# Weight transfers at time 0, first one-hot rows by VectorE, high halves and 1/z products by GpSimd, z transfers on the SyncE queue

## The chip, the cores and the metric

The kernel runs on one core of one Trainium2 chip. The metric is the device time in microseconds (us) of one execution; smaller is better. Times quoted are medians of the timed runs. "Span" is the length of the one execution that was profiled. It is about 2 us below that run's time, and it can be one of the faster or slower runs.

Engine names: PE is TensorE, ACT is ScalarE, DVE is VectorE, POOL is GpSimd and SP is SyncE. A "q" after the name (SPq) means the engine's instruction queue, which issues transfers.

## The reference

Attention restricted to clusters, followed by an MLP with SiLU. Every query and key is assigned to one of 16 centroids of its head, and a query sees only keys of its own cluster.

```python
# q, k, v: (4, 8, 768, 64); centroids: (8, 16, 64); w_in: (512, 2048); w_out: (2048, 512), all float32
q_assign = argmax(einsum('bhsd,hcd->bhsc', q_n, c_n), -1)      # q_n, k_n, c_n: normalised
k_assign = argmax(einsum('bhsd,hcd->bhsc', k_n, c_n), -1)
mask = q_assign[:, :, :, None] == k_assign[:, :, None, :]
scores = where(mask, (q @ k.T) / sqrt(64), -1e9)
attn = exp(scores - max(scores)); attn /= sum(attn) + 1e-9
x = (attn @ v) as (3072, 512)                                   # 3072 tokens
h = x @ w_in;  g = h * sigmoid(h);  out = g @ w_out
```

## The kernel before

The mask is part of the score matmul. Q and K are turned so that the 64 features lie on partitions 0 to 63, and 16 more partitions (64 to 79) hold the one-hot cluster rows. One matmul over 80 partitions gives the score plus a large constant where the clusters agree. Each number is split into two f16 numbers, a high half and a low half (`hl`), and the two are transposed together: for the first four pairs of heads by PE, for the later pairs by a transposing DMA.

The work is a list of 144 slots. A slot is one score tile (`st`), one exp (`P`) and later one product with V (`pv`). The 16 pairs of heads, four per batch, take nine slots each. MoE matmuls (`ph`, `po`) start once a batch has finished a third of its tokens; they fill PE from then on. Each engine carries out its instructions in program order, and so does each queue that issues DMAs.

```python
def cast_v(p):                                   # V to f16, by GpSimd
    for h in range(2):
        nc.gpsimd.tensor_copy(vts[p % NV][:, :, h, 0:D], natvs[p][:, h]...)

def split(p, t, part, eng=nc.vector):            # t: 0 for q, 1 for k
    if part == 0:                                # L94: high halves
        eng.tensor_scalar(out=hl[:, :, 0, :], in0=nat, scalar1=128.0, scalar2=None, op0=ALU.mult)
    else:                                        # L97: low halves
        nc.vector.scalar_tensor_tensor(out=hl[:, :, 1, :], in0=nat, scalar=128.0, in1=hl[:, :, 0, :], ...)

def turn_dma(p, t):                              # L107
    nc.sync.dma_start_transpose(abt_of(p)[:, t], hls.pop((p, t)).rearrange("p a c d -> p (a c d)"))

# ... logits (PE), route_a to route_d (DVE): transpose, max, compare, transpose, scale -> one-hot rows oh
def route_e(pl):                                 # L176: one-hot rows into place, by DMA
    for a, p in enumerate(pl):
        for h in range(2):
            for t in range(2):
                nc.sync.dma_start(ab[D : D + HC, h, :], oh[g : g + HC, :])

# the sum of exps (z) of one slot triple: to 32 partitions, 1/z, to DRAM, broadcast to 64 partitions
def z_out(n):    nc.gpsimd.dma_start(zt, osbs[n][D : D + 1]...)
def z_recip(n):  nc.vector.reciprocal(rz, zts.pop(n)); nc.gpsimd.dma_start(rzd..., rz)
def z_bcast(n):  nc.gpsimd.dma_start(rzb..., rzs.pop(n).to_broadcast([64, 2 * UQ]))
def z_mul(n, p, u):                              # L235: products with 1/z
    for h in range(2):
        nc.vector.tensor_tensor(out=xts[c]..., in0=osb[0:D, h, :], in1=rzb[:, h, :], op=ALU.mult)

# ... the weights: 16 casting DMAs (f32 in DRAM, f16 in SBUF) on GpSimd's queue, one per two slots
for n in range(2):
    for r in range(NR):
        wld.append(lambda r=r, o=o: nc.gpsimd.dma_start(win_s[:, r, o], win_v[:, r, o]))
for g in range(NFB // 2):
    wld.append(lambda g=g: nc.gpsimd.dma_start(wout_s[:, 2 * g : 2 * g + 2], wout_v[:, 2 * g : 2 * g + 2]))
# ...
for n, fn in enumerate(wld):
    at(1 + 2 * n, fn)
```

The softmax here doesn't subtract the row's maximum and nothing guards it: scores larger than these inputs give would overflow.

Of the kernel before, what the change touches and what calls it, by code (L numbers as in the profile page):

```python
# [17 lines left out]
def kernel(  # L18
# [41 lines left out]

    wh = const.tile([128, HB, 2, 32], f16, name="wh")
    wl = const.tile([128, HB, 2, 32], f16, name="wl")
    NV = 6
    vts = [const.tile([128, NJ, 2, 128], f16, name=f"vt{n}") for n in range(NV)]

# [14 lines left out]
    def load_v(p):  # L80
        b, r = divmod(p, HB)
        natv = mp.tile([128, 2, NJ * D], f32, name="natv", bufs=2)
        nc.sync.dma_start(natv, v[b, 2 * r : 2 * r + 2].rearrange("h (p j) d -> p h (j d)", j=NJ))
        natvs[p] = natv
# [2 lines left out]
        for h in range(2):  # L87
            nc.gpsimd.tensor_copy(vts[p % NV][:, :, h, 0:D], natvs[p][:, h].rearrange("p (j d) -> p j d", d=D))

    def split(p, t, part, eng=nc.vector):  # L90
        nat = nats[p, t].rearrange("p h (j d) -> p (h j) d", d=D)
        if part == 0:
            hl = hls[p, t] = mp.tile([128, 2 * NJ, 2, D], f16, name="hl", bufs=3)
            eng.tensor_scalar(out=hl[:, :, 0, :], in0=nat, scalar1=128.0, scalar2=None, op0=ALU.mult)  # L94
        else:
            hl = hls[p, t]
            nc.vector.scalar_tensor_tensor(  # L97
                out=hl[:, :, 1, :], in0=nat, scalar=128.0, in1=hl[:, :, 0, :], op0=ALU.mult, op1=ALU.subtract
            )
# [76 lines left out]
                    nc.sync.dma_start(ab[D : D + HC, h, :], oh[g : g + HC, :])  # L176


    K = D + HC

    def qk(n, s, p, u):
# [28 lines left out]

    def z_out(n):
        zt = mp.tile([32, 16], f32, name="zt", bufs=3)
        nc.gpsimd.dma_start(zt, osbs[n][D : D + 1].rearrange("o h x -> o (h x)").rearrange("o (p i) -> o p i", p=32))  # L213
        zts[n] = zt

    def z_recip(n):
        rz = mp.tile([32, 16], f32, name="rz", bufs=2)
        nc.vector.reciprocal(rz, zts.pop(n))  # L218
        rzd = dr.tile([1, 2 * UQ], f32, name="rzd", bufs=4)
        nc.gpsimd.dma_start(rzd.rearrange("o (p i) -> (o p) i", p=32), rz)  # L220
        rzs[n] = rzd

    def z_bcast(n):
        rzb = mp.tile([64, 2, UQ], f32, name="rzb", bufs=4)
        nc.gpsimd.dma_start(rzb.rearrange("p h x -> p (h x)"), rzs.pop(n).to_broadcast([64, 2 * UQ]))  # L225
        rzbs[n] = rzb

    def z_mul(n, p, u):
        b, r = divmod(p, HB)
        c = b * U + u  # L230
        if c not in xts:
            xts[c] = mp.tile([128, NR, UQ], f16, name="xt", bufs=5)
        osb, rzb = osbs.pop(n), rzbs.pop(n)
        for h in range(2):
            nc.vector.tensor_tensor(  # L235
                out=xts[c][D * h : D * h + D, r, :], in0=osb[0:D, h, :], in1=rzb[:, h, :], op=ALU.mult
            )

# [52 lines left out]
    def centroid_rest(craw):  # L291
# [12 lines left out]
            nc.vector.tensor_scalar(out=ch2[:, n, :], in0=chh, scalar1=OHV, scalar2=None, op0=ALU.mult)  # L304
        for n in range(2):
            nc.vector.scalar_tensor_tensor(out=cl2[:, n, :], in0=cn, scalar=OHV, in1=ch2[:, n, :], op0=ALU.mult, op1=ALU.subtract)
        for src, dst in ((ch2, wh), (cl2, wl)):
            pt = ps.tile([128, 128], f16, name="pt", tag="moe", bufs=3)
            nc.tensor.transpose(pt, src.rearrange("p n d -> p (n d)"), ident)
            pt4 = pt.rearrange("p (r h c) -> p r h c", h=2, c=HC)  # L310
            for h in range(2):
                nc.vector.tensor_copy(dst[:, :, h, HC * h : HC * h + HC], pt4[:, :, h])


    units = []
# [11 lines left out]
        events.setdefault(slot, []).append(fn)  # L327


    nc.vector.memset(zbias, 0.0)  # L330
    nc.vector.memset(bias32, -32.0)
    craw = load_centroids()
    for p in range(2):
        for t in range(2):
            load(p, t)
    make_identity(nc, ident)
    nc.vector.memset(wh, 0.0)
    nc.vector.memset(wl, 0.0)
    for vt in vts:
        nc.gpsimd.memset(vt[:, :, :, D:128], 1.0)  # L340
    load_v(0)
    AC, VE = nc.scalar, nc.vector
    centroid_norm(craw)
    for t in range(2):
        split(0, t, 0, VE)
        split(0, t, 1)
# [1 line left out]
        for h in range(2):  # L348
            turn_pe(0, t, h, AC)
    for t in range(2):  # L350
        split(1, t, 0)
    centroid_rest(craw)
    logits([0])
    for t in range(2):
        load(2, t)
    load_v(1)
    split(1, 0, 1)
    route_a([0])
    route_b([0])
    route_c([0])  # L360
    route_d([0])
    route_e([0])
    cast_v(0)
    split(1, 1, 1)
    for t in range(2):
        for h in range(2):
            turn_pe(1, t, h, AC)

    wld = []
    for n in range(2):  # L370
        for r in range(NR):
            o = slice(n * DF // 2, (n + 1) * DF // 2)
            wld.append(lambda r=r, o=o: nc.gpsimd.dma_start(win_s[:, r, o], win_v[:, r, o]))
    for g in range(NFB // 2):
        wld.append(lambda g=g: nc.gpsimd.dma_start(wout_s[:, 2 * g : 2 * g + 2], wout_v[:, 2 * g : 2 * g + 2]))


    def route(pl, x):
# [25 lines left out]
    route([1], 1)  # L404
    front_pe(2, 2)
    front_pe(3, 9)
    at(0, lambda: cast_v(1))
    at(0, lambda: (load(3, 0), load(3, 1), load_v(2)))
    at(3, lambda: load_v(3))
    at(6, lambda: cast_v(2))  # L410
    at(8, lambda: cast_v(3))
    for n, fn in enumerate(wld):
        at(1 + 2 * n, fn)
    for b in range(1, B):
        front([b * HB, b * HB + 1], 36 * b - (3 if b == 1 else 8))
        front([b * HB + 2, b * HB + 3], 36 * b + (4 if b == 1 else 2))
# [88 lines left out]
```

## Time and profile before

| | before |
|---|---|
| time, median of the first 3 runs (range) | 393.85 us (393.36 to 396.67) |
| span of the profiled run | 390.8 us |
| first MoE matmul | 116.2 us |
| from there to the end | 274.6 us |
| exp of slot 0, 17, 24, 36 starts at | 23.8, 52.3, 77.8, 105.4 us |
| first eight transposes: first issue to last landing | 55.5 to 102.7 us |

Windows of the kernel before. Each row is a stretch of time: its length, the busy time (and instruction count) of PE, PE's weight loads, DVE, ACT and POOL, then PE's granted clock, the mean busy share of the 16 DMA engines, and GB/s.

```profile
core 0: us, PE busy (x) PEld busy (x) DVE busy (x) ACT busy (x) POOL busy (x), PEclk, DMA share, GB/s
0.00:52.00 52.00, 34.19 (x278) 24.05 (x278) 33.51 (x70) 28.93 (x32) 17.98 (x36) 0.80 0.58 149
52.00:78.00 26.00, 10.38 (x72) 7.05 (x72) 15.61 (x28) 7.96 (x9) 9.45 (x16) 0.73 1.13 208
78.00:116.00 38.00, 24.36 (x207) 17.11 (x206) 22.62 (x41) 18.91 (x18) 14.96 (x28) 0.86 0.87 156
106.00:380.00 274.00, 265.79 (x2116) 198.16 (x2115) 179.81 (x334) 175.43 (x204) 66.67 (x131) 0.99 0.38 103
```

In the last row PE is busy 266 of 274 us at a granted clock of 0.99: that part is bound by PE, and faster transfers could win at most the 8 us in which PE is idle. In the second row PE is busy only 10 of 26 us, while the DMA engines have no free time (a share above 1 means that packets' times overlap on an engine).

What PE waited for in the kernel before (total us, times, longest wait):

```profile
PE st L186 <- DMA abt<-oh: 24.3, 10, 11.6
PE ptt L113 <- DVE hl L97: 11.0, 3, 6.2
```

The largest wait is for the DMA that puts the one-hot rows into place. But that DMA is small, and it is only the last step of a chain. The chain of work that ended last (start, us, what), cut to its long pieces in the front:

```profile
2.67 6.06 DMA nat_93<-in_k_dram
...
18.70 3.88 DMA abt<-oh
...
53.25 3.68 DMA abt<-oh
...
71.56 3.11 SPq L107
74.72 5.06 DMA nat_789<-in_q_dram
79.79 13.02 DMA abt<-hl
```

`abt<-hl` is a transposing DMA. It took 13.0 us to land, and SyncE needed 3.1 us to issue one. The group of the first eight of these transposes, in the same trace (durations are SyncE's issue in ns; the second line is from issue to landing):

```profile
L107 SPq DMA_TRANSPOSE abt<-hl x8: 2073/4082/6230, 55.5 to 96.1; - x8
...
DMA to landing us min/median/max: 6.6/10.4/13.0
```

So the front can be read as three pieces that add up to the first MoE matmul: the stretch of the eight transposes begins (55.5 us), lasts (47.2 us), and 13.5 us later the first MoE matmul runs (116.2 us).

Of the work that the change moves, the products with 1/z are one group. Its columns are the number of instructions, busy us and mean ns, and the idle time before them with its cause.

```profile
L235 DVE TENSOR_TENSOR xt<-osb,rzb 64x256 f16<-64x256 f32 x96 | 40.6, 423 | 3.3 <-DMA rzb<-rzd 2.6
```

The high halves (L94) stand in the listing one by one, each with its own buffer; the median takes VectorE 0.55 us, and one takes 0.56 us in the chain.

### The profile page before, as it was taken

To read this page: it belongs to the slowest core of one execution; us is meant where nothing else is said; L and a number is where in the kernel's file an instruction comes from. 1 tells how busy PE (TensorE), PEld (TensorE's weight loads), DVE (VectorE), ACT (ScalarE), POOL (GpSimd) and SP (SyncE) were. 2 spreads that over 40 slices of the span, in tenths; PEclk is the share of its full clock that TensorE was granted. 3 is DMA by queue.
4 is the path that set the end of the run, shared out by engine and by line. 5 is a ranking of instruction groups with operands and counts; after the bars stand their busy time and mean duration, and the time that the engine had idled before them with its cause. 6 is when DMAs were issued, how large, how long until landed. Compare 5 with 4: busy or idle time off the path is not lost.

```text
span 390.8 us, 6883 instructions
## 1 busy us (share of the span) xinstructions
PE 336.5 (86%) x2658; PEld 245.4 (63%) x2658; DVE 248.0 (63%) x464; ACT 226.0 (58%) x255; POOL 106.0 (27%) x204
## 2 busy tenths in 40 slices
PE   2476965183849999999999999999999999999995
PEld 2345644162538877677777776777776777776572
DVE  6827577465554796796755786785845364555661
ACT  5157655054456776574776766665667666663350
POOL 5305162353420314223213133133221313122200
PEclk9668798588887999999999999999999999999999
DMA  7663589999716179654034598645120111111111
GB/s 250 128 200 70 118 164 219 199 243 181 145 45 206 30 190 267 136 138 102 20 118 154 137 245 216 137 101 96 49 68 16 55 42 49 48 43 54 68 42 55
DMA packets 65072, 47.35 MB, mean 121 GB/s; under 512 B 44048, under 2 KB 59408, under 8 KB 65040
## 3 DMA queue, kind: packets, MB, share of 16 engines
q1 hardware_dynamic: 56336, 36.22, 36.7%
q0 software_dynamic: 8704, 10.69, 13.5%
q8 instruction: 21, 0.34, 0.4%
q14 instruction: 11, 0.09, 0.1%
HBM read 33.59 MB, written 6.39 MB: 102 GB/s over the span
## 4 chain that ended last, share of the span: by engine, by line
PE 69%; DVE 12%; DMA 10%; issue 4%; SPq 3%; ACT 2%; DVEq 0%; ACTq 0%
PE ph L246 20%; PE po L260 19%; PE pv L201 14%; PE st L186 13%; DMA abt<-oh 4%; DMA abt<-hl 3%; PE psL L130 3%; DVE hl L97 2%; DMA nat_93<-in_k_dram 2%; DVE oht L155 1%; DVE mx L148 1%; SPq L176 1%; DMA nat_789<-in_q_dram 1%; DVE xt L235 1%; DVE ohu L164 1%
## 5 line engine op out<-in xcount | busy, mean ns | idle before, releaser
L190 ACT ACTIVATE P<-st,bias_70 128x1024 f16<-128x1024 f32 x144 | 158.1, 1115 | 93.8 <-PE st L186 93.1
L186 PE MATMUL st<-abt 80*128 80x256 f16 x576 | 92.2, 284 | 25.8 <-DMA abt<-oh 24.3
L251 DVE SCALAR_TENSOR_TENSOR gt<-tn,ph 128x512 f16<-128x512 f32 x96 | 64.9, 678 | 76.8 <-ACT tn L250 76.5
L246 PE MATMUL ph<-xt,win_s 128*128 128x256 f16 x768 | 99.4, 275 | 2.5 <-DVE lt L140 0.9
L260 PE MATMUL po<-wout_s,gt 128*128 128x512 f16 x384 | 96.0, 379 | 0.0
L250 ACT ACTIVATE tn<-ph,zbias 128x512 f32<-128x512 f32 x96 | 65.6, 684 | 47.4 <-PE ph L246 45.7
L186 PEld LDWEIGHTS <-abt 80*128 80x128 f16 x576 | 56.8, 101 | 46.4 <-DMA abt<-oh 27.0
L246 PEld LDWEIGHTS <-win_s 128*128 128x128 f16 x768 | 75.8, 99 | 15.2 <-issue 3.8
L220 POOL DMA_DIRECT2D rzd<-rz x48 | 25.1, 522 | 158.0 <-DVE rz L218 151.4
L260 PEld LDWEIGHTS <-gt 128*128 128x128 f16 x384 | 37.4, 97 | 28.5
L207 DVE COPY osb<-pv 128x512 f32<-128x512 f32 x48 | 32.5, 676 | 21.2 <-PE pv L201 21.2
L225 POOL DMA_DIRECT2D rzb<-rzd x48 | 25.1, 522 | 68.3 <-DMA rzd<-rz 68.3
L235 DVE TENSOR_TENSOR xt<-osb,rzb 64x256 f16<-64x256 f32 x96 | 40.6, 423 | 3.3 <-DMA rzb<-rzd 2.6
L213 POOL DMA_DIRECT2D zt<-osb x48 | 24.0, 501 | 30.4 <-DVE osb L207 30.1
L201 PE MATMUL pv<-P,vt_77 128*128 128x256 f16 x108 | 17.3, 304 | 5.5 <-DVE osb L207 5.5
L263 DVE TENSOR_SCALAR ot<-po 128x512 f32<-128x512 f32 x24 | 16.1, 669 | 7.8 <-PE po L260 7.8
L113 PE MATMUL ptt<-ident,hl 128*128 128x128 f16 x96 | 9.9, 266 | 11.0 <-DVE hl L97 11.0
L201 PEld LDWEIGHTS <-vt_77 128*128 128x128 f16 x108 | 11.7, 108 | 10.0 <-issue 5.7
L201 PE MATMUL pv<-P,vt_75 128*128 128x256 f16 x108 | 16.1, 289 | 0.0
L116 ACT COPY abt<-ptt 128x768 f16<-128x768 f16 x12 | 9.2, 805 | 11.5 <-PE ptt L113 11.5
L113 PEld LDWEIGHTS <-hl 128*128 128x128 f16 x96 | 8.0, 121 | 12.6 <-DVE hl L97 12.0
L140 DVE STREAM_TRANSPOSE lt<-psL 128x512 f32<-128x512 f32 (+1 forms) x10 | 7.1, 709 | 13.8 <-PE psL L130 13.8
(128 smaller groups left out, 272.3 us busy)
## 6 DMA issues: line engine op xcount, KB each, us to landing
natv<-in_v_dram SPq DMA_DIRECT2D x16, 384.0 KB, 5.7
rzb<-rzd POOLq DMA_DIRECT2D x48, 128.0 KB, 2.9
out_dram<-ot SPq DMA_DIRECT2D x24, 256.0 KB, 2.2
win_s<-in_moe_w_in_dram POOLq DMA_DIRECT2D x8, 256.0 KB, 5.2
wout_s<-in_moe_w_out_dram POOLq DMA_DIRECT2D x8, 256.0 KB, 8.8
abt<-oh SPq DMA_DIRECT2D x64, 24.0 KB, 2.0
zt<-osb POOLq DMA_DIRECT2D x48, 2.0 KB, 2.1
rzd<-rz POOLq DMA_DIRECT2D x48, 2.0 KB, 1.8
```

What stands on the lines that cost most here:

```text
L186: nc.tensor.matmul(st[:, a, h, :], ab[0:K, 1, h, ts(2 * s + a, 128)], ab[0:K, 0, h, ts(u, UQ)], start=True, stop=True)
L190: nc.scalar.activation(out=P, in_=st, func=AF.Exp, bias=bias32, scale=ESC)
L201: nc.tensor.matmul(po[:, h, :], vts[p % NV][:, 2 * s + a, h, :], P[:, a, h, :], start=(s == 0 and a == 0 and h == 0), stop=(s == 2 and a = ...
L207: nc.vector.tensor_copy(osb, po)
L213: nc.gpsimd.dma_start(zt, osbs[n][D : D + 1].rearrange("o h x -> o (h x)").rearrange("o (p i) -> o p i", p=32))
L220: nc.gpsimd.dma_start(rzd.rearrange("o (p i) -> (o p) i", p=32), rz)
L225: nc.gpsimd.dma_start(rzb.rearrange("p h x -> p (h x)"), rzs.pop(n).to_broadcast([64, 2 * UQ]))
L235: nc.vector.tensor_tensor(out=xts[c][D * h : D * h + D, r, :], in0=osb[0:D, h, :], in1=rzb[:, h, :], op=ALU.mult)
L246: nc.tensor.matmul(ph[:, e, :], win_s[:, r, ts(2 * f + e, 128)], xts[c][:, r, :], start=(r == 0), stop=(r == NR - 1))
L250: nc.scalar.activation(out=tn, in_=ph, func=AF.Tanh, bias=zbias, scale=0.5)
L251: nc.vector.scalar_tensor_tensor(out=gts[c][:, 2 * f : 2 * f + 2, :], in0=tn, scalar=1.0, in1=ph, op0=ALU.add, op1=ALU.mult)
L260: nc.tensor.matmul(po, gts[c][:, fc, ts(s, 128)], wout_s[:, fc, :], start=(fc == 0), stop=(fc == NFB - 1))
```

## The change

The intent is to take the weight transfers out of the saturated stretch (part 1), to take a DMA out of the way to the first scores (part 2), to relieve VectorE by giving elementwise work to GpSimd (part 3), and to free GpSimd's queue of the z transfers so that it can do that work (part 4).

```diff
-    def split(p, t, part, eng=nc.vector):
+    def split(p, t, part, eng=nc.gpsimd):                    # part 3
@@ ...
+    def route_first():                                       # part 2: rows of pair 0
+        ...   # logits with 32 columns per (q/k, head), of which 16 are used; transpose; max; compare; transpose
+        for h in range(2):
+            for t in range(2):
+                g = 64 * h + 32 * t
+                nc.vector.tensor_scalar(out=ab[D : D + HC, h, :], in0=ohu[g : g + HC, :], scalar1=OHV, ...)
@@ z_out, z_recip, z_bcast
-        nc.gpsimd.dma_start(...)
+        nc.sync.dma_start(...)                               # part 4
@@ z_mul
-            nc.vector.tensor_tensor(
+            nc.gpsimd.tensor_tensor(                         # part 3
@@ main
     centroid_norm(craw)
+    for r in range(NR):                                      # part 1: eight DMAs of twice the size
+        nc.gpsimd.dma_start(win_s[:, r], win_v[:, r])
+    for g in range(NFB // 4):
+        nc.gpsimd.dma_start(wout_s[:, 4 * g : 4 * g + 4], wout_v[:, 4 * g : 4 * g + 4])
@@ ...
     for t in range(2):
         load(2, t)
     load_v(1)
+    for t in range(2):
+        load(3, t)
+    split(1, 0, 0, AC)                                       # pair 1's high halves by ScalarE
+    split(1, 1, 0, AC)
     centroid_rest(craw)
     split(1, 0, 1)
-    route_a([0]) ... route_e([0])
+    route_first()
     cast_v(0)
+    for vt in vts[2:]:
+        nc.gpsimd.memset(vt[:, :, :, D:128], 1.0)
+    cast_v(1)
+    load_v(2)
+    load_v(3)
@@ ...
-    for n, fn in enumerate(wld):
-        at(1 + 2 * n, fn)
```

Two smaller things go with the four parts: ScalarE makes pair 1's high halves, and pair 3's q and k are loaded earlier.

More of the change, by code (lines that the diff above doesn't have):

```diff
@@ L62 @@
     wl = const.tile([128, HB, 2, 32], f16, name="wl")
+    w0 = const.tile([128, 2, 32], f16, name="w0")
     NV = 6
@@ L93, in split @@
             hl = hls[p, t] = mp.tile([128, 2 * NJ, 2, D], f16, name="hl", bufs=3)
-            eng.tensor_scalar(out=hl[:, :, 0, :], in0=nat, scalar1=128.0, scalar2=None, op0=ALU.mult)
+            if eng is nc.scalar:
+                nc.scalar.mul(hl[:, :, 0, :], nat, 128.0)
+            else:
+                eng.tensor_scalar(out=hl[:, :, 0, :], in0=nat, scalar1=128.0, scalar2=None, op0=ALU.mult)
         else:
@@ L176, in route_e @@
                     nc.sync.dma_start(ab[D : D + HC, h, :], oh[g : g + HC, :])
+    oht0 = mp.tile([128, S], f16, name="oht", bufs=1)
+    def route_first():
+        tl = []
+        for lo, hi in ((0, 512), (512, 768)):
+            psL = ps.tile([128, 512], f32, name="psL", tag="moe", bufs=3)
+            for i, w in enumerate((wh, wl)):
+                for h in range(2):
+                    for t in range(2):
+                        g = 64 * h + 32 * t
+                        ab = abts[0][:, t].rearrange("p (h j) c -> p h (j c)", h=2)
+                        nc.tensor.matmul(
+                            psL[g : g + 32, 0 : hi - lo], w0[:, i] if h else w[:, 0, 0], ab[:, h, lo:hi],
+                            start=(i == 0), stop=(i == 1),
+                        )
+            tl.append(psL)
+        lt = mp.tile([128, S], f32, name="lt", bufs=1)
+        nc.vector.transpose(lt[:, 0:512], tl[0])
+        nc.vector.transpose(lt[:, 512:768], tl[1][:, 0:256])
+        l3 = lt.rearrange("p (a c) -> p a c", c=32)[:, :, 0:HC]
+        mx = mp.tile([128, S // 32], f32, name="mx0")
+        nc.vector.tensor_reduce(out=mx, in_=l3, axis=AX.X, op=ALU.max)
+        oht = oht0
+        nc.vector.tensor_tensor(
+            out=oht.rearrange("p (a c) -> p a c", c=32)[:, :, 0:HC], in0=l3,
+            in1=mx.unsqueeze(2).to_broadcast([128, S // 32, HC]), op=ALU.is_ge,
+        )
+        ohu = mp.tile([128, S], f16, name="ohu", bufs=1)
+        nc.vector.transpose(ohu, oht)
+        for h in range(2):
+            for t in range(2):
+                g = 64 * h + 32 * t
+                ab = abts[0][:, t].rearrange("p (h j) c -> p h (j c)", h=2)
+                nc.vector.tensor_scalar(
+                    out=ab[D : D + HC, h, :], in0=ohu[g : g + HC, :], scalar1=OHV, scalar2=None, op0=ALU.mult
+                )
     K = D + HC
@@ L212, in z_out @@
         zt = mp.tile([32, 16], f32, name="zt", bufs=3)
-        nc.gpsimd.dma_start(zt, osbs[n][D : D + 1].rearrange("o h x -> o (h x)").rearrange("o (p i) -> o p i", p=32))
+        nc.sync.dma_start(zt, osbs[n][D : D + 1].rearrange("o h x -> o (h x)").rearrange("o (p i) -> o p i", p=32))
         zts[n] = zt
@@ L219, in z_recip @@
         rzd = dr.tile([1, 2 * UQ], f32, name="rzd", bufs=4)
-        nc.gpsimd.dma_start(rzd.rearrange("o (p i) -> (o p) i", p=32), rz)
+        nc.sync.dma_start(rzd.rearrange("o (p i) -> (o p) i", p=32), rz)
         rzs[n] = rzd
@@ L224, in z_bcast @@
         rzb = mp.tile([64, 2, UQ], f32, name="rzb", bufs=4)
-        nc.gpsimd.dma_start(rzb.rearrange("p h x -> p (h x)"), rzs.pop(n).to_broadcast([64, 2 * UQ]))
+        nc.sync.dma_start(rzb.rearrange("p h x -> p (h x)"), rzs.pop(n).to_broadcast([64, 2 * UQ]))
         rzbs[n] = rzb
@@ L306, in centroid_rest @@
             nc.vector.scalar_tensor_tensor(out=cl2[:, n, :], in0=cn, scalar=OHV, in1=ch2[:, n, :], op0=ALU.mult, op1=ALU.subtract)
-        for src, dst in ((ch2, wh), (cl2, wl)):
+        for i, (src, dst) in enumerate(((ch2, wh), (cl2, wl))):
             pt = ps.tile([128, 128], f16, name="pt", tag="moe", bufs=3)
@@ L312, in centroid_rest @@
                 nc.vector.tensor_copy(dst[:, :, h, HC * h : HC * h + HC], pt4[:, :, h])
+            nc.vector.tensor_copy(w0[:, i, 0:HC], pt4[:, 0, 1])
     units = []
@@ L327, in at @@
         events.setdefault(slot, []).append(fn)
+    AC, VE = nc.scalar, nc.vector
     nc.vector.memset(zbias, 0.0)
@@ L335 @@
             load(p, t)
+    load_v(0)
     make_identity(nc, ident)
@@ L338 @@
     nc.vector.memset(wl, 0.0)
-    for vt in vts:
+    nc.vector.memset(w0, 0.0)
+    nc.vector.memset(oht0, 0.0)
+    for vt in vts[0:2]:
         nc.gpsimd.memset(vt[:, :, :, D:128], 1.0)
-    load_v(0)
-    AC, VE = nc.scalar, nc.vector
     centroid_norm(craw)
+    for r in range(NR):
+        nc.gpsimd.dma_start(win_s[:, r], win_v[:, r])
+    for g in range(NFB // 4):
+        nc.gpsimd.dma_start(wout_s[:, 4 * g : 4 * g + 4], wout_v[:, 4 * g : 4 * g + 4])
     for t in range(2):
@@ L350 @@
     for t in range(2):
-        split(1, t, 0)
-    centroid_rest(craw)
-    logits([0])
-    for t in range(2):
         load(2, t)
     load_v(1)
-    split(1, 0, 1)
-    route_a([0])
-    route_b([0])
-    route_c([0])
-    route_d([0])
-    route_e([0])
-    cast_v(0)
+    for t in range(2):
+        load(3, t)
+    split(1, 0, 0, AC)
+    split(1, 1, 0, AC)
+    centroid_rest(craw)
+    split(1, 0, 1)
+    route_first()
+    cast_v(0)
+    for vt in vts[2:]:
[3 more added lines that the diff above has]
+    load_v(3)
     split(1, 1, 1)
@@ L367 @@
             turn_pe(1, t, h, AC)
-    wld = []
-    for n in range(2):
-        for r in range(NR):
-            o = slice(n * DF // 2, (n + 1) * DF // 2)
-            wld.append(lambda r=r, o=o: nc.gpsimd.dma_start(win_s[:, r, o], win_v[:, r, o]))
-    for g in range(NFB // 2):
-        wld.append(lambda g=g: nc.gpsimd.dma_start(wout_s[:, 2 * g : 2 * g + 2], wout_v[:, 2 * g : 2 * g + 2]))
     def route(pl, x):
@@ L406 @@
     front_pe(3, 9)
-    at(0, lambda: cast_v(1))
-    at(0, lambda: (load(3, 0), load(3, 1), load_v(2)))
-    at(3, lambda: load_v(3))
     at(6, lambda: cast_v(2))
     at(8, lambda: cast_v(3))
-    for n, fn in enumerate(wld):
-        at(1 + 2 * n, fn)
     for b in range(1, B):
```

## The prediction

> **What bounds the kernel now.** The table of busy time by stretch splits the span in two. From 120 us PE is busy 263 of 271 us at full clock: bound by PE. Before 116 us (first MoE matmul) it is busy 69 us, 47 idle. In the table of waits the largest idle is for abt<-oh (the one-hot rows' DMA): 24.3 us, 11.6 of it at 64-76 us. PE's work after 116 us is the same in both kernels, so what shortens the front shortens the whole.
>
> **What holds the front.** From 60 to 100 us the DMA share is 1.2: saturated. By the DMA packets of the trace, three weight DMAs (256 KB written each) kept the queue full from 15.5 to 22 us, 2 us each, so all 16 cost about 32 us. Eight (w_out) were issued at 53-97 us, among eight transposes (2 us of DMA each when alone). Estimate for 55-103 us: weights 16, transposes 16, loads 10, 1/z broadcasts 6 = 48 us: all of it.
>
> **The change.**
> 1. Weights at time 0: the 32 us now compete with the first loads. The Trainium skill ("DMA: Bandwidth & Descriptors", Queues, rings and completion order) says that each DMA engine takes queue rows in turn, by packet. The trace agrees roughly: at 38-42 us both queues got about half. So pair 1's q/k land about 3 us later (11-12 instead of 8.7), weights end near 46 us, and pair 1's one-hot DMA is slowed by 1-2 us. In return 16 us leave the saturated stretch, and the 3 us wait at 53-56 us goes. Gain about 13 us.
> 2. First one-hot rows by VectorE: removes DMA issue and landing at 18.0-22.6 us and halves the reduce and compare (0.95 us each); adds four copies (0.36 us each, as oh<-ohu). But PE must still turn pair 1 first. First st matmul at about 19.5 instead of 22.6: gain 3 us.
> 3. VectorE loses xt (40.6 us) and the high halves (0.55 us x 28): in the front 2-4 us of the routing chain, later off the chain. GpSimd gains them: high halves about 1.0 us (cast of 384 columns: 0.5 us); products by the skill ("GPSIMD Engine Reference", Elementwise — side-by-side cycle accounting, 2.6 cycles per element) an estimated 0.65-0.75 us, against 0.42 on VectorE. It loses 74 us of z issues.
> 4. z transfers on SyncE: 144 issues of about 0.5 us join, in order, transposes (1.3-6 us each in the front) and one-hot DMAs (0.55 us each); GpSimd's products, waiting, block its next high halves. This takes back 2-4 us in the front. After 120 us slack hides it. At the tail the last product ended just as PE needed it: loss 0-1 us.
>
> **Sum.** First MoE matmul at about 97 us; rest unchanged at 275 us; span 372 us; timed about 375 us (timed runs are 2-3 us above the span). Range 365 to 386. Chances: faster 0.85, within 2% 0.13, slower 0.02.
>
> **What would show it.** 1: no weight packets after 50 us; transposes landing in under 5 us in the front; the wait for abt<-oh under 10 us. 2: first st matmul at 18-21 us. 3: xt on GpSimd 0.6-0.9 us, VectorE busy near 190 us. 4: SyncE's waits before z transfers grow; PE over 95% busy after the first MoE matmul.
>
> **What would make it wrong.** Weight packets starving the first loads (start later than 23 us); SyncE's order making z latency pace the front, so that freed DMA time is not used; GpSimd products far over 1 us; or ScalarE's exp (1.1 us a slot) as the next floor, for a larger gain.

## The result, and the profile after

The ratio is the mean time of the changed kernel's fast runs over that of the kernel before's fast runs of the same rounds, so it is not quite the ratio of the medians.

| | before | after |
|---|---|---|
| time, median of 4 runs (range) | 395.26 (393.36 to 397.34) | 381.84 (381.10 to 382.93) |
| ratio, 95% interval | | 0.9662 [0.9597, 0.9726] |
| span | 390.8 | 379.8 |
| first MoE matmul | 116.2 | 105.9 |
| from there to the end | 274.6 | 273.9 |
| exp of slot 0, 17, 24, 36 | 23.8, 52.3, 77.8, 105.4 | 21.9, 52.3, 70.2, 94.8 |
| the eight transposes begin | 55.5 | 57.6 |
| they last | 47.2 | 34.8 |
| from there to the first MoE matmul | 13.5 | 13.6 |

The kernel became 3.4% faster. In the profiled pair, 10.3 of the 11.0 us between the spans are in the front, as predicted. The table already shows an oddity: slot 17 starts at 52.3 us in both, so the whole gain comes after it.

The windows of the kernel after:

```profile
core 0: us, PE busy (x) PEld busy (x) DVE busy (x) ACT busy (x) POOL busy (x), PEclk, DMA share, GB/s
0.00:52.00 52.00, 33.46 (x278) 24.69 (x278) 31.80 (x71) 30.50 (x34) 30.45 (x36) 0.93 0.81 193
52.00:78.00 26.00, 15.28 (x113) 10.69 (x112) 13.97 (x20) 13.20 (x13) 15.66 (x12) 0.87 0.91 206
78.00:116.00 38.00, 28.18 (x236) 20.92 (x236) 18.99 (x31) 20.43 (x21) 23.40 (x26) 0.87 0.49 119
106.00:380.00 274.00, 266.21 (x2105) 196.68 (x2103) 139.93 (x232) 170.14 (x198) 103.02 (x110) 0.99 0.37 104
```

The DMA share rose from 0.58 to 0.81 in the first row and fell in the second and third: the weights moved from there to here. PE did 113 instead of 72 matmuls from 52 to 78 us. In the first row PE got no further (278 matmuls in both). The last row is the same as before for PE, although VectorE has 40 us less to do there. The granted clock also differs in the front (0.80 on average up to the first MoE matmul before, 0.91 after), but PE's busy time there fell only from 69.1 to 66.8 us, so by this a faster PE accounts for about 2 of the 10.3 us at most.

What PE waited for in the kernel after, its first eight transposes, and the group of the products:

```profile
PE ptt L118 <- DVE hl L102: 17.6, 4, 5.9
...
PE st L229 <- DMA abt<-oh: 12.1, 6, 5.4
```

```profile
L112 SPq DMA_TRANSPOSE abt<-hl x8: 1312/1572/2852, 57.6 to 86.6; - x8
...
DMA to landing us min/median/max: 4.0/5.1/5.9
```

```profile
L278 POOL TENSOR_TENSOR xt<-osb,rzb 64x256 f16<-64x256 f32 x96 | 76.5, 797 | 146.6 <-DMA rzb<-rzd 136.1
```

The transposes land in half the time, and SyncE is held 1.6 instead of 4.1 us by one. The wait for the one-hot rows halved. In its place another wait grew, from 11.0 to 17.6 us: PE's own transposes (`ptt`) wait for the halves.

The chain of the kernel after shows where those come from (start, us, what):

```profile
3.17 17.91 DMA natv<-in_v_dram
21.14 0.95 POOL vt_76 L90 x2
...
24.81 4.32 issue
30.10 2.13 POOL hl L99
32.25 1.59 DVE hl L102
33.89 0.82 PE ptt L118 x6
```

The chain of the front now begins with a load of V that took 17.9 us, and goes over GpSimd. The 4.3 us of "issue" are GpSimd's wait for the next V, as its timeline shows (start, us; idle time and its cause in brackets):

```profile
29.15 0.95 POOL L90 CAST vt_77<-natv 128x384 f16<-128x384 f32 x2 [4.34 <-DMA natv<-in_v_dram]
30.07 2.14 POOL L99 TENSOR_SCALAR hl<-nat_166 128x768 f16<-128x768 f32 x1
32.20 2.12 POOL L99 TENSOR_SCALAR hl<-nat_168 128x768 f16<-128x768 f32 x1
```

GpSimd works in order. It could not make pair 2's high halves before it had cast pair 1's V, which landed at 29.1 us, though pair 2's q had landed at 23.6. Each half then took 2.1 us. Slot 6 started at 35.7 us, where it had been 32.1 us in the kernel before, and the 1.9 us won at slot 0 were gone.

### The profile page after: what moved, and what is told of

Its sections match the earlier page's. It is cut to its first block, busy times and chain, and to the rows that moved or that the text cites. A ratio compares the mean times of both kernels' runs of the same rounds, so it can differ in the third digit from the quotient of the medians.

```text
span 379.8 us, 6956 instructions
## 1 busy us (share of the span) xinstructions
PE 333.1 (88%) x2658; PEld 245.0 (64%) x2658; DVE 201.1 (53%) x345; ACT 227.6 (60%) x257; POOL 166.7 (44%) x176
## 3 DMA queue, kind: packets, MB, share of 16 engines
q0 software_dynamic: 2688, 4.19, 6.0%
## 4 chain that ended last, share of the span: by engine, by line
PE 71%; DMA 11%; DVE 6%; issue 4%; POOL 3%; SPq 3%; ACT 1%; POOLq 0%; DVEq 0%; ACTq 0%
PE ph L289 22%; PE po L303 21%; PE st L229 13%; PE pv L244 13%; DMA natv<-in_v_dram 5%; DMA abt<-hl 3%; POOL hl L99 2%; DVE hl L102 1%; PE psL L135 1%; SPq L181 1%; DMA zt<-osb 1%; DMA abt<-oh 1%; DMA rzb<-rzd 1%; DVE osb L250 1%; SPq L79 1%
## 5 line engine op out<-in xcount | busy, mean ns | idle before, releaser
L278 POOL TENSOR_TENSOR xt<-osb,rzb 64x256 f16<-64x256 f32 x96 | 76.5, 797 | 146.6 <-DMA rzb<-rzd 136.1
L294 DVE SCALAR_TENSOR_TENSOR gt<-tn,ph 128x512 f16<-128x512 f32 x96 | 65.7, 685 | 103.6 <-ACT tn L293 103.5
L229 PE MATMUL st<-abt 80*128 80x256 f16 x576 | 91.4, 283 | 13.8 <-DMA abt<-oh 12.1
L250 DVE COPY osb<-pv 128x512 f32<-128x512 f32 x48 | 32.3, 673 | 12.4 <-PE pv L244 12.4
L118 PE MATMUL ptt<-ident,hl 128*128 128x128 f16 x96 | 10.5, 277 | 17.7 <-DVE hl L102 17.6
L261 DVE RECIPROCAL rz<-zt 32x16 f32<-32x16 f32 x48 | 11.2, 233 | 19.8 <-DMA zt<-osb 13.2
L135 PE MATMUL psL<-abt,wh 128*32 128x512 f16 (+1 forms) x120 | 11.5, 345 | 7.9 <-DMA abt<-hl 5.5
L244 PE MATMUL pv<-P,vt_78 128*128 128x256 f16 x108 | 16.1, 289 | 1.4 <-DVE osb L250 1.4
L244 PE MATMUL pv<-P,vt_76 128*128 128x256 f16 x108 | 15.9, 287 | 0.0
L244 PE MATMUL pv<-P,vt_79 128*128 128x256 f16 x108 | 15.1, 277 | 0.0
L244 PE MATMUL pv<-P,vt_77 128*128 128x256 f16 x108 | 14.7, 272 | 0.0
```

What stands on the lines that cost most here:

```text
L118: nc.tensor.transpose(pt[:, j, :], hl[:, h * NJ + j].rearrange("p c d -> p (c d)"), ident)
L135: nc.tensor.matmul(psL[g : g + 32, 0 : hi - lo], w[:, p % HB, h], ab[:, h, lo:hi], start=(n == 0), stop=(n == 3))
L229: nc.tensor.matmul(st[:, a, h, :], ab[0:K, 1, h, ts(2 * s + a, 128)], ab[0:K, 0, h, ts(u, UQ)], start=True, stop=True)
L244: nc.tensor.matmul(po[:, h, :], vts[p % NV][:, 2 * s + a, h, :], P[:, a, h, :], start=(s == 0 and a == 0 and h == 0), stop=(s == 2 and a = ...
L250: nc.vector.tensor_copy(osb, po)
L278: nc.gpsimd.tensor_tensor(out=xts[c][D * h : D * h + D, r, :], in0=osb[0:D, h, :], in1=rzb[:, h, :], op=ALU.mult)
```

## The experiments

The questions were: which part makes the gain, and why is it 13 and not 19 us? The texts name theories by letters. In short: A says that the early weights make the gain by emptying the transposes' stretch, and that the missing part is lost behind GpSimd's slow, in-order high halves. B says that SyncE, with the z transfers in its order, paces the front. D asks what VectorE's relief is worth by itself. G says that the early weights gain only together with part 2. H says that GpSimd's work, done beside VectorE's, is what slows the start. The other letters mark variants of these, and the texts give the numbers that each expects.

All twelve kernels computed the right result. A row of the table splits the front as above: start of the eight transposes, their length, the time from there to the first MoE matmul. "Ratio" is to the kernel before in the same rounds. The kernel before varies between chips (medians of its fast runs 392.4 to 395.8; eight of its runs were slow and are left out of the ratios), so compare ratios, not medians, between rows. The columns of the front come from one profiled run each. Spans of one kernel differ by up to 5.6 us between the fast runs (c_gpsimd_clear_of_first_rows, 374.5 to 380.1), so a difference of 1 or 2 us in these columns is only a hint.

| kernel | median us | ratio [95%] | slot 0 | slot 17 | start | length | then | first MoE |
|---|---|---|---|---|---|---|---|---|
| before | 395.26 | 1 | 23.8 | 52.3 | 55.5 | 47.2 | 13.5 | 116.2 |
| after | 381.84 | 0.9662 [0.9597, 0.9726] | 21.9 | 52.3 | 57.6 | 34.8 | 13.6 | 105.9 |
| a_high_on_vector | 382.92 | 0.9742 [0.9674, 0.9810] | 21.2 | 53.0 | 58.1 | 36.0 | 14.7 | 108.8 |
| a_products_on_vector | 384.56 | 0.9789 [0.9728, 0.9850] | 22.1 | 52.5 | 57.8 | 35.2 | 15.5 | 108.6 |
| a_z_on_gpsimd_queue | 382.43 | 0.9734 [0.9657, 0.9811] | 21.0 | 51.6 | 55.3 | 36.2 | 15.6 | 107.1 |
| a_weights_spread | 383.95 | 0.9783 [0.9674, 0.9891] | 22.2 | 48.1 | 53.3 | 39.8 | 14.2 | 107.3 |
| b_weights_first | 392.71 | 1.0005 [0.9930, 1.0079] | 35.1 | 64.6 | 67.9 | 35.0 | 14.5 | 117.4 |
| b_z_on_sync | 393.82 | 1.0026 [0.9957, 1.0094] | 24.1 | 57.0 | 62.1 | 38.0 | 14.9 | 115.0 |
| b_gpsimd_work | 390.17 | 0.9921 [0.9842, 0.9999] | profile slow | | | | | |
| a_both_on_vector | 386.02 | 0.9831 [0.9760, 0.9902] | 21.2 | 52.2 | 57.3 | 35.0 | 14.9 | 107.2 |
| a_weights_after_v0 | 381.82 | 0.9675 [0.9608, 0.9743] | 24.6 | 52.0 | 56.6 | 36.5 | 14.9 | 107.9 |
| a_weights_two_parts | 382.22 | 0.9716 [0.9656, 0.9777] | 23.7 | 51.6 | 56.6 | 33.6 | 15.6 | 105.8 |
| a_first_rows_by_dma | 392.03 | 0.9954 [0.9897, 1.0011] | 36.1 | 61.4 | 66.2 | 35.3 | 14.0 | 115.6 |
| c_gpsimd_clear_of_first_rows | 379.12 | 0.9588 [0.9489, 0.9688] | 20.3 | 48.6 | 53.6 | 35.4 | 15.6 | 104.6 |

Names with a_ undo or move a part of the changed kernel, those with b_ do one part alone on the kernel before, and c_ is a new version. Differences of two or three us between the a_ kernels lie within each other's intervals; I draw nothing from them alone.

### a_high_on_vector: GpSimd's high halves back on VectorE

```diff
-    def split(p, t, part, eng=nc.gpsimd):
+    def split(p, t, part, eng=nc.vector):
```

> The changed kernel with the high halves back on VectorE (0.55 us each there, 2.13 us on GpSimd). Theory A: these 2.13 us stand on the chain of waits before the first MoE matmul (7.7 us of it are POOL hl), so this is 3 to 5 us faster than the changed kernel (about 378 us against 381.8), first MoE matmul near 102 us instead of 106. Theory B (SyncE, which now carries z, loads, transposes and one-hot rows in order, paces the front): within 1 us of the changed kernel.

It was no faster than the changed kernel, so A's second half missed as it stood. The cause it named was there and went away: PE no longer waited at slot 6 (slots 6 and 7 ran by 31.4 us). But the time was lost again three slots later, before slot 9: the wait for one-hot rows was larger than in the changed kernel (12.1 us).

```profile
PE st L229 <- DMA abt<-oh: 16.4, 7, 6.5
```

Removing one wait exposed the next, and slot 17 stood at 53.0 us.

### a_products_on_vector: GpSimd's products back on VectorE

```diff
-            nc.gpsimd.tensor_tensor(
+            nc.vector.tensor_tensor(        # in z_mul
```

> The changed kernel with the products with 1/z back on VectorE (0.42 us each there, 0.80 us on GpSimd). Theory A: they stand on no chain, so within 1.5 us of the changed kernel. Theory C: in GpSimd's order they hold up the high halves behind them while they wait for the broadcast, so taking them away gains 2 to 4 us.

384.6 us, 2.7 us slower by the median, so both expectations missed (within 1.5 us, or faster). The intervals only just fail to overlap (0.9726 and 0.9728 are their near ends), and they come from different calls. The start and the length of the transposes' stretch hardly moved (57.8 and 35.2 us); in the profiled run the time is lost after it (15.5 us instead of 13.6). Why is left open.

### a_z_on_gpsimd_queue: the z transfers back on GpSimd's queue

```diff
-        nc.sync.dma_start(zt, ...)          # and the two others of z
+        nc.gpsimd.dma_start(zt, ...)
```

> The changed kernel with the z transfers back on GpSimd's queue. Theory B (SyncE paces the front): 3 us or more faster than the changed kernel, one-hot rows issued earlier. Theory A: no gain; GpSimd's order now makes the high halves wait behind transfers that wait for VectorE, so 0 to 5 us slower.

382.4 us: the time did not change. SyncE, with 144 issues fewer, did not let the front run faster, so theory B falls, and the 2 to 4 us that the prediction charged for step 4 do not show in the time.

### a_weights_spread: the weights as before, all else as after

```diff
-    for r in range(NR):
-        nc.gpsimd.dma_start(win_s[:, r], win_v[:, r])
-    for g in range(NFB // 4):
-        nc.gpsimd.dma_start(wout_s[:, 4 * g : 4 * g + 4], wout_v[:, 4 * g : 4 * g + 4])
@@ ...
+    for n, fn in enumerate(wld):            # the 16 transfers of the kernel before
+        at(1 + 2 * n, fn)
```

> The changed kernel with the weights spread over the slots as before. Theory A: the whole gain of slots 17 to 24 (7.6 us) came from weights leaving the stretch of the transposes, while at the start they cost about 4 us by holding the first loads back: this is 3 to 8 us slower than the changed kernel, with the first st matmul before 18 us and the gap at slots 5 to 8 gone. Rival: the gain came from VectorE's relief and the first rows, so this is within 2 us of the changed kernel or faster.

This is the most telling of the first four. The early weights were meant to be the heart of the change, worth 13 us; without them the first MoE matmul ran at 107.3 us, only 1.4 us later than with them. This profile is the fastest of four runs that range from 381.8 to 387.2 us; by the median the version is 2.1 us slower, by the ratio 1.2%, with intervals that overlap. So the early weights bring at most a few us here, and neither expectation (3 to 8 us slower, or within 2) is settled. The part of the first that placed the first score matmul before 18 us missed: slot 0 started at 22.2. Its stretch:

```profile
L112 SPq DMA_TRANSPOSE abt<-hl x8: 1302/2190/3298, 53.3 to 87.2; - x8
...
DMA to landing us min/median/max: 3.9/6.1/8.0
```

The split says why: the early weights begin the stretch 4.3 us later (53.3 to 57.6) and shorten it by 5.0 us (39.8 to 34.8). The two nearly cancel. Against the kernel before, the stretch had shrunk by 7.4 us without early weights. The trace gives a part of the reason. Before, the last of w_in went out at 49.9 us and all eight of w_out at 53.0 to 97.0 us, into the stretch. Here w_in was out by 34.8 us and two of w_out by 49.1, and w_out's transfers landed in 5.1 us (median) where it had been 8.8. Why they went out earlier is tested by itself in b_z_on_sync. The weight transfers in flight during the stretch are eight, six, four and none in the kernel before, here, in b_z_on_sync and in the changed kernel, and its length 47.2, 39.8, 38.0 and 34.8 us. That is an order, not a proportion, so the count is not the whole of it; the rest is left open.

### b_weights_first: the early weights alone

```diff
-    for vt in vts:
+    for vt in vts[0:2]:
         nc.gpsimd.memset(vt[:, :, :, D:128], 1.0)
+    for r in range(NR):
+        nc.gpsimd.dma_start(win_s[:, r], win_v[:, r])
+    for g in range(NFB // 4):
+        nc.gpsimd.dma_start(wout_s[:, 4 * g : 4 * g + 4], wout_v[:, 4 * g : 4 * g + 4])
+    ...                                      # the other four memsets
@@ ...
-    for n, fn in enumerate(wld):
-        at(1 + 2 * n, fn)
```

> The kernel before with the weight DMAs alone moved to time 0 (placed and cut as in the changed kernel). The runs so far give the changed kernel's stretch of eight transposes 34.8 us from first issue to last landing against 47.2 us before, and 39.8 us with the weights spread again. Theory A (weights among the transposes made the stretch long): the stretch falls to 35 to 40 us; but the first loads are starved, slots 0 to 17 end 2 to 5 us later; total 3 to 8 us faster than before. Theory D (VectorE's load made it long): stretch 44 us or more, total no faster than before.

No gain at all: 1.0005 [0.9930, 1.0079]. The stretch shrank by 12.2 us, much as in the changed kernel (12.4), and the start grew by 12.4 us. So theory A had the stretch right, and its gain of 3 to 8 us missed. The chain of this kernel, cut to its two long pieces in the start, and its transposes:

```profile
2.68 15.14 DMA nat<-in_k_dram
...
29.55 4.61 DMA abt<-oh
```

```profile
DMA to landing us min/median/max: 5.1/6.1/8.2
```

In the kernel before, that load of k took 6.1 us in the chain. Now it landed at 17.8, VectorE stood before pair 1's high half in program order and made pair 0's one-hot rows only afterwards, and their DMA, beside the weights, landed at 34.2.

### b_z_on_sync: the z transfers on SyncE alone

```diff
-        nc.gpsimd.dma_start(zt, ...)        # and the two others of z
+        nc.sync.dma_start(zt, ...)
```

> The kernel before with the z transfers alone moved to SyncE. Theory A: within 2 us of before, or slower by up to 4 us from SyncE's order. Rival E (on GpSimd's queue weights and z transfers stood behind one another and broke into the transposes): stretch of the transposes 3 us or more shorter than 47.2 us.

No gain in time (1.0026), but a side effect that only the rival E had foreseen. GpSimd's queue no longer stood waiting for z, so the weights behind it were issued earlier: 12 of the 16 by 37.5 us, where before the twelfth went out at 69.0 us. The stretch shrank by 9.2 us. But nine of those transfers were issued between 30.6 and 37.5 us, just when pair 1's one-hot rows were due (piece of the chain of this kernel):

```profile
36.50 6.08 DMA abt<-oh
```

and the stretch began 6.6 us later. With the last piece 1.4 us longer, the first MoE matmul came 1.2 us earlier than in the kernel before (115.0 us); the rest of this run, the slowest of its four, took 278.4 us instead of 274.6, which is not explained. So both part 1 and part 4 pull the weights out of the stretch, and each, alone, gives most or all of the time back in the start.

### b_gpsimd_work: the high halves and the products on GpSimd alone

```diff
-    def split(p, t, part, eng=nc.vector):
+    def split(p, t, part, eng=nc.gpsimd):   # pair 1's stay on VectorE
@@ z_mul
-            nc.vector.tensor_tensor(
+            nc.gpsimd.tensor_tensor(
```

> The kernel before with the high halves of pairs 2 to 15 and the products alone moved to GpSimd (weights, z transfers and first rows as before). Theory D (VectorE's relief gave the gain): 6 us or more faster than before, stretch of the transposes below 42 us. Theory A: within 3 us of before, possibly slower, as GpSimd's order now mixes these with waits for z.

The ratio is 0.9921 [0.9842, 0.9999]: 0.8% faster, 1.6% at most. VectorE's busy time fell from 248 to 205 us, and that alone bought little: theory D, which asked for 6 us or more, falls. The profiled run was slow, so its stretches are not compared.

### a_both_on_vector: all of part 3 undone

```diff
-    def split(p, t, part, eng=nc.gpsimd):
+    def split(p, t, part, eng=nc.vector):
@@ z_mul
-            nc.gpsimd.tensor_tensor(
+            nc.vector.tensor_tensor(
```

> The changed kernel with both high halves and products back on VectorE (what stays: weights at time 0, first rows, z on SyncE, earlier loads). Theory D: the gain goes, 388 us or more. Theory A: 381 to 386 us, as with each of them alone (382.9 and 384.6).

386.0 us, ratio 0.9831 against the changed kernel's 0.9662: part 3 as a whole is worth about 1.7% by the ratios and 1.1% by the medians, at the edge of what A expected (381 to 386 us). The two intervals do not overlap (0.9726 and 0.9760 are their near ends), but they come from different calls. VectorE was busy 247 us and GpSimd only 31. The profiled run was the fastest of the five (383.5 us), and its front was 1.3 us later than the changed kernel's (107.2 us); the other four runs were 2.4 to 2.7 us slower than this one and have no profile.

### a_first_rows_by_dma: part 2 undone, with the early weights kept

```diff
-    route_first()
+    logits([0])
+    route_a([0])
+    ...
+    route_e([0])
```

> The changed kernel with pair 0's one-hot rows again by DMA on SyncE (as the kernel before routes them). Theory G (the early weights gain only because the first rows no longer wait for a DMA: with the weights alone slot 0 slid to 35 us): these four DMAs stand behind the starved loads of pairs 2 and 3 on the same queue, slot 0's exp at 28 to 36 us, timed 6 to 12 us slower than the changed kernel. Rival (the two parts gain independently; prediction's step 2 gave the rows 3 us): slot 0 at 24 to 26 us, timed within 4 us of the changed kernel.

392.0 us: nearly the whole gain went. Slot 0 started at 36.1 us. The chain of this kernel:

```profile
3.69 20.60 DMA nat<-in_q_dram
...
24.37 10.83 DMA abt<-oh
```

The last of the four DMAs of the rows was issued at 24.4 us, when an earlier load in SyncE's order (pair 2's q) had landed, and then took 10.8 us beside the weights; the first, issued at 19.1 us, took 15.3. The stretch itself was as in the changed kernel (35.3 us). Theory G holds: with the weights early, the first rows by VectorE are worth 9.7 us (115.6 to 105.9), not the 3 us that the prediction gave them, and the early weights without them are worth nothing (b_weights_first). Part 2 alone on the kernel before was not run.

### a_weights_after_v0: weights issued when pair 0's V has been cast

```diff
-    for r in range(NR): ...                 # the eight weight DMAs at time 0
     cast_v(0)
+    for r in range(NR): ...                 # the same eight, here
```

> The changed kernel with the eight weight DMAs behind the cast of pair 0's v in GpSimd's order, so that pairs 0 and 1 load alone. Theory A (the stretch gained 12 us, but the starved first loads gave back what the start should have gained): slot 0's exp at 18 to 20 us (21.9 in the changed kernel), slot 17's at 46 to 49 (52.3), stretch of the transposes still about 35 us, first MoE matmul at 99 to 103, timed 375 to 379 us. Rival F (slots 6 to 17 are held by GpSimd's slow high halves and order, not by the weights): slot 17 at 51 or later, timed 380 or more.

The loads came early again (the last of the first eight by 13.7 us) as intended, but slot 0 started at 24.6 us, later than with the weights at time 0. It missed its expectation, and slot 17 (52.0 us) and the time (381.8 us) fell where the rival, F, had put them: F says that GpSimd's slow high halves and its order hold slots 6 to 17. The timelines of GpSimd and VectorE show a cost that I had not in my sum:

```profile
14.47 3.02 POOL L410 DMA_DIRECT2D wout_s<-in_moe_w_out_dram  x4
17.41 2.86 POOL L412 MEMSET vt<- 128x768 f16 x4
20.14 1.29 POOL L90 CAST vt<-natv 128x384 f16<-128x384 f32 x2
```

```profile
14.56 6.50 DVE L217 TENSOR_SCALAR abt<-ohu 16x768 f16<-16x768 f16 x4
```

VectorE's four copies of the first rows took 6.5 us. In the changed kernel they took 0.35 us each:

```profile
L217 DVE TENSOR_SCALAR abt<-ohu x4: 350/352/355, 16.8 to 17.9; 16x768 f16<-16x768 f16 x4
```

One of the four ran from 16.4 to 20.5 us, across the end of one DMA issue of GpSimd, another, four memsets and the start of a cast. The Trainium skill ("SBUF — State Buffer", Who interferes with whom) says that a VectorE instruction in a two-port mode, which a `tensor_scalar` can enter, contends with GpSimd for a port pair that one of them holds for its whole instruction while the other fully blocks. No view here shows the mode or the ports. The trace agrees that a VectorE instruction can be held up beside GpSimd. It shows more than one instruction's worth of it: the longest GpSimd instruction there lasted 0.8 us, the copy 4.1.

### a_weights_two_parts: w_in after pair 0's V, w_out in slots 8 to 14

```diff
     cast_v(0)
+    for r in range(NR):
+        nc.gpsimd.dma_start(win_s[:, r], win_v[:, r])
@@ ...
+    for g in range(NFB // 4):
+        at(8 + 2 * g, lambda g=g: nc.gpsimd.dma_start(wout_s[:, 4 * g : 4 * g + 4], ...))
```

> The changed kernel with the four w_in DMAs behind the cast of pair 0's v and the four w_out DMAs at slots 8, 10, 12 and 14. Theory A: as with all weights behind pair 0's v or better, since pair 1's one-hot DMA and pair 2's loads meet fewer weights: slot 17's exp at 45 to 48 us, stretch 34 to 37 us, timed 374 to 378 us. Rival F: slot 17 at 51 or later, 380 or more. If w_out still runs at slot 17 it lengthens the stretch and part of the gain goes.

382.2 us, as the changed kernel, where 374 to 378 had been expected; slot 17 (51.6 us) again stood where F had put it. The four copies took 0.84 to 1.36 us each, and slot 0 started at 23.7 us: fewer of GpSimd's instructions beside them, a smaller loss. It pointed at the last run.

### c_gpsimd_clear_of_first_rows: GpSimd idle while VectorE makes the first rows

```diff
-    def split(p, t, part, eng=nc.gpsimd):
+    def split(p, t, part, eng=nc.vector):
@@ main
-    for vt in vts[0:2]:
+    for vt in vts:                          # all memsets before the loads land
         nc.gpsimd.memset(vt[:, :, :, D:128], 1.0)
-    for r in range(NR): ...                 # the eight weight DMAs at time 0
     cast_v(0)
-    for vt in vts[2:]: ...
+    for r in range(NR):
+        nc.gpsimd.dma_start(win_s[:, r], win_v[:, r])
@@ ...
+    def w_out():                            # w_out once a product with V is there
+        nc.gpsimd.tensor_copy(gate, osbs[1][0:1, 0, 0:1])
+        for g in range(NFB // 4): ...
+    at(8, w_out)
```

> The changed kernel with all memsets of the value tiles at the start, the four w_in DMAs behind the cast of pair 0's v, the four w_out DMAs behind the second unit's osb (a copy of one element gates them), and the high halves on VectorE, so that GpSimd has little to do while VectorE copies the first rows. Theory H (in the two runs with the weights behind v0 GpSimd's memsets, casts and high halves stretched these four copies from 0.35 us each to 0.8-4.1, and that hid what the unstarved loads gained): the four copies take under 2.5 us together (6.5 and 4.8 there), slot 0's exp at 18.5 to 20.5 us, slot 17's at 45 to 48.5, first MoE matmul at 99 to 104, timed 375 to 379.5 us. If slots 6 to 17 have another pacer (theory F), slot 17 stays at 51 or later and the time at 380 or more.

The four copies were back at full speed (1.45 us in all), which confirms H for them. The weights' own traffic is not the cause: w_in's transfers, issued at 10.7 to 12.4 us and landed by 27.2, ran beside these copies too. VectorE's timeline:

```profile
15.42 1.45 DVE L217 TENSOR_SCALAR abt<-ohu 16x768 f16<-16x768 f16 x4
```

Slot 0 started at 20.3 us, slot 17 at 48.6 and the transposes' stretch at 53.6, 4.0 us before the changed kernel's. The time was 379.1 us and the ratio 0.9588 [0.9489, 0.9688], 4% faster than the kernel before. Its interval overlaps that of the changed kernel, so a gain over that one is not shown. This version moves the weights, the memsets and the high halves at once, so it does not say how much of slot 17's gain belongs to H and how much to F; with the high halves alone back on VectorE (a_high_on_vector) slot 17 stood at 53.0 us. Slot 17 and the first MoE matmul (104.6) lay just beyond the bounds; the profiled run was the slowest of the four (381.9 us). Of the 3.7 us won by slot 17 only 1.3 were left at the first MoE matmul; why the later pieces (35.4 and 15.6 us, instead of 34.8 and 13.6) grew is left open.

## Why the prediction was right, and where it was off

The time was predicted as 375 us, within 365 to 386; it was 381.8. The direction and the place were right. The missing 6.8 us are all in the front: the first MoE matmul came at 105.9 instead of 97 us, while the rest, predicted as 275, took 273.9 us. That the time fell within the range is in part luck: the largest term, 13 us for step 1, came out at 0 alone, and step 2, given as 3 us, came out at 9.7 beside it.

**What bounds the kernel: right.** After the first MoE matmul PE is busy 267.3 of 274.6 us before and 266.3 of 273.9 after, although VectorE lost 36 us of work there (176.2 to 139.9). What shortens the front shortens the whole.

**Step 1, mechanism: right.** Clearing the weights from the stretch shortened the eight transposes from 47.2 to 34.8 us; 48 to 32 had been estimated. No weight landed after 39.4 us, the transposes landed in 5.1 us ("under 5" had been written), and PE's wait for the one-hot rows halved (24.3 to 12.1 us; "under 10" had been written). The weights' queue of the changed kernel:

```profile
q0 software_dynamic: 2688, 4.19, 6.0%
```

That is 22.8 us of all 16 engines (0.060 x 379.8), not the estimated 32. Summing the packets of w_out alone (2048 of 1 KB) in the two traces gives 14.9 us before and 12.3 after, so the 16 us for it were nearly right, and the stretch lost 12.4.

**Step 1, net gain of 13 us: wrong. This is the term that failed.** Measured alone it gained 0 us (b_weights_first); put on top of the other three parts it brought the first MoE matmul forward by 1.4 us in the profiled runs, and the time by 2.1 us by the medians (a_weights_spread against the changed kernel). The prediction charged the start with about 3 us, since "at 38-42 us both queues got about half", and 1 to 2 us for a slower one-hot DMA. In the changed kernel pair 1's k landed at 17.6 us, not 11 to 12, and pair 1's V at 29.1. The DMA queues of the changed kernel from 8 to 18 us (packets, MB, share of the 16 engines' time), with q0 the weights and q1 the loads:

```profile
q0 software_dynamic: 469, 1.72, 85.3%
q1 hardware_dynamic: 467, 0.67, 21.6%
```

The Trainium skill ("DMA: Bandwidth & Descriptors", Queues, rings and completion order) says that an engine takes the queue rows in turn, packet by packet. The trace agrees in the count, almost to the packet: 469 against 467. (The page's packet holds several descriptors; the trace does not show whether its own packets are the same thing.) But w_in's packets are 3.7 KB as written (1.72 MB / 469) and the loads' 1.4 KB (0.67 / 467), and one of w_in's kept an engine 0.29 us, one of the loads' 0.074 (share x 16 engines x 10 us / packets). An equal share of packets was 85% against 22% of the time. From 20 to 30 us, where w_out with its 1 KB packets was moving, a packet of the weights took 0.094 us, one of the loads 0.075. The loads then had the larger part of the bytes, but still the smaller part of the time:

```profile
q0 software_dynamic: 1094, 1.09, 64.0%
q1 hardware_dynamic: 1095, 1.58, 51.1%
```

I had taken turns by packet for halves of the time. The window that the prediction leaned on (kernel before, 38 to 42 us) was no test of turns: its packets were 191 of the weights' queue to 518 of the loads', and in its first us no weight packet moved. Whether w_in cut into smaller packets, or w_out sent first, would save the start was not tried.

**Step 2, 3 us: right in itself, too small in company.** The first score matmul came at 20.8 instead of 22.6 us (19.5 predicted). But with the early weights on the queue the same step is worth 9.7 us, because the DMA that it replaces takes 10.8 us there instead of 3.9. It is what lets step 1 pay at all. The prediction added the steps as if each could be costed alone.

**Step 3: sizes off.** The high half took GpSimd 2.13 us, not 1.0, and the product 0.80, not 0.65 to 0.75. VectorE's low half, made beside GpSimd's next high half, took 1.59 us in the chain above, where 0.95 is usual. VectorE's busy time fell from 248 to 201 us (190 predicted). In the front the relief was not the 2 to 4 us: with both back on VectorE the first MoE matmul came only 1.3 us later, in the fastest run of that version. The slow high half, behind a late V in GpSimd's order, took back at slot 6 what slot 0 had won, so that slot 17 stood at 52.3 us in both kernels. Mending that one wait (a_high_on_vector) only moved it to slot 9.

**Step 4: the cost was not there, and the use was another.** The z transfers on SyncE cost nothing that the time shows (a_z_on_gpsimd_queue: no change in the other direction). Their move frees GpSimd's queue, and the weights behind it then go out earlier; this is a second way to the same saving (stretch 38.0 us in b_z_on_sync). That is my reading of why the changed kernel without early weights still has most of the gain. It is argued from the times of issue in these traces; the version with the weights spread and z on GpSimd's queue, all else as after, was not run.

**The sum.** The parts as the prediction wrote them are 13 + 3 + 3 - 3 = 16 us, which gives 100 and not 97 for the first MoE matmul: three us of the miss were a slip of addition. The rest shows in the split of the front. With the estimated 32 us of stretch and the 13.5 after it, 97 needed a stretch that began at 51.5 us; it began at 57.6, 6.1 late, and lasted 2.8 us longer. 6.1 + 2.8 is the 8.9 that were missed. Of the 6.1, 4.3 are the early weights' by the one profile of a_weights_spread.

## What to carry to other kernels

Moving transfers out of a saturated stretch pays only by the difference between what that stretch saves and what the transfers cost where they land; measure both ends, and expect that queues which share the DMA engines can split packets evenly, as here, so that the one whose packets take longer gets most of the time. Parts of a change that act on the same shortage cannot be summed: here two of them gained nothing alone, and removing a third, which had been costed at 3 us, took back 10. An engine given extra work in program order also delays what stood behind it, and a busy GpSimd can slow a small copy of VectorE's more than tenfold (4.10 us instead of 0.35 here, in the worst of four).

## What the Trainium skill lacked or had wrong

- "DMA: Bandwidth & Descriptors" (Queues, rings and completion order): the turn by packet fits the counts (469 packets against 467), but the page does not draw the consequence that a queue's share of the time then follows how long its packets take: 85.3% against 21.6% of the time with packets of 0.29 and 0.074 us (3.7 and 1.4 KB).
- "DMA: Bandwidth & Descriptors" (Rules for kernel authors) says that a casting DMA is issued from GpSimd, and I found no rate for it: 4.19 MB written as f16 from f32 took 22.8 us of all 16 engines. Nor did I find what a transposing DMA costs beside other traffic: landing in 10.4 us (median) beside the weights, 5.1 without them.
- "SBUF — State Buffer" (Who interferes with whom) says that, when VectorE is in a two-port mode, the later of VectorE and GpSimd blocks for the other's instruction. The runs show one VectorE instruction held up over a whole row of GpSimd instructions: one 16x768 f16 copy took 4.10 us across seven of them (the first and last in part), of at most 0.82 us each, and 0.35 us with GpSimd idle.
- "GPSIMD Engine Reference" (Engine selection) calls one-input elementwise work on GpSimd roughly line-rate. A tensor_scalar from f32 to f16 of 128x768 took 2.13 us there and 0.56 on VectorE, 3.8 times as long. The estimate that I drew from the page's two-input figure (Elementwise — side-by-side cycle accounting), 0.65 to 0.75 us, was nearer: 0.797.
